# Start-up of a recurrent attention and two MLP layers on one core: set-up, gate rows and sigmoids in other places of the order

## The chip, the cores and the metric
One core of a Trainium2 chip runs the kernel. The metric is the device time of one execution in microseconds (us); the time before is 479.1 us, the median of three runs from 477.7 to 480.66. TensorE is called PE, VectorE DVE, ScalarE ACT, GpSimd POOL, and SyncE, which issues all the transfers here, SP.

## The reference, cut to what matters
For 2 batches, 8 heads, 768 time steps and head size 40, a gated recurrence gives `y`; its 1536 rows of 320 numbers pass through two MLP layers with 2048 hidden units each.

```python
for t in range(S):                                   # attention
    m_new = np.maximum(f_gate[:, :, t] + m, i_gate[:, :, t])
    f_stab, i_stab = np.exp(f_gate[:, :, t] + m - m_new), np.exp(i_gate[:, :, t] - m_new)
    C = f_stab * C + i_stab * outer(v_t, k_t)
    n = f_stab * n + i_stab * k_t
    y[:, :, t] = sigmoid(o_gate[:, :, t]) * (C @ q_t) / np.maximum(np.abs(n @ q_t), 1.0)
x = y.transpose(0, 2, 1, 3).reshape(B * S, H * D)
h = x @ w_in;   x = (h - np.tanh(h)) @ w_out         # layer 0
h = x @ w_in2;  out = (h * np.tanh(softplus(h))) @ w_out2   # layer 1
```

The inputs are float32, but the weights come as 64-bit numbers, which the kernel itself converts.

## The kernel before, in words
**Attention** is done in chunks of 128 time steps: 6 chunks of 2 batches give 12 token tiles j, two tiles to a block. `attention(j)` is a generator that yields between its steps: two halves of exponents of decays (Exp, L304) from PSUM, a POOL product `wv` (L316), two halves of scores (PE L321, DVE L323), the state product `it` for later chunks, the value product `pv` (L341), and then on DVE the denominator (L349 to L351) and the gated output in `xo` (L353, L354). `xo` must hold the sigmoid of the output gate by then. `transpose_x` turns two finished tiles into `xT` (PE L246, ACT L248, DVE L249), the input of layer 0.

**The gates** are rows of 16 partitions (one for each batch and head) by 768 steps: `n_t` and `i_t` (called a in the change) come from DVE scans (L396, L404). They are split into two float parts in `nr` (L434 on ACT, L435 on DVE), from which small transfers (L269, L275) fill rows of `md` and `sd`, the operands of the decay product for chunks past the first (L301). `sd`, `md` and the state `C` are first set to constants by POOL. `u_t` (L442 on POOL) and its Exp give `uT` and `dec` through PE.

**Weights** come in 16 pieces f for each layer. `conv_w` converts one: DVE L175, L176, ACT L177, DVE L178 (the third pass), ACT L179, and then L181 and L182 for the low part, on POOL for the first two pieces and on DVE for the others. The first three pieces of layer 0 have buffers of their own; later ones share three raw buffers, so a new piece is loaded when an older one is converted.

**Layer 0** goes in tiles of two weight pieces: `mm1` (L493), `tile1` (two tanh and Square on ACT, L519, L520 and L522 on DVE, the split into `gh` and `gl`), `mm2` (L552 to L554). For the first block pieces 0 to 7 are converted one after the other while the tiles use them; `conv_to` asks for them ahead. `ahead` advances the attention of the next blocks between tiles.

**Order**: a planner orders each engine's instructions from the order in the program and its own time estimates. `after(x)` adds an order on one engine behind the instructions in `x`, with no wait of its own. `session(c0, c1)` puts output-gate sigmoids behind every Exp and Tanh so far (`texp`) and then a dummy Exp (L626), behind which later Exp and Tanh come (`tbl`). So it holds ACT for two table loads and the sigmoids. Session (0, 2) is in the first block; session (2, 6) stands in `attend`, at the seventh step of the second block. PE runs dummy products (`spin`, L592) in gaps of the start.

Of the kernel before, what the change touches and what calls it, by code (L numbers as in the profile page):

```python
# [8 lines left out]
F32 = mybir.dt.float32  # L9
# [16 lines left out]
def kernel(  # L26
# [11 lines left out]
    nc = tc.nc  # L38
# [89 lines left out]

    texp, tbl, dls = [], [], []

    spq, cvd, hold = [], [], []

    def after(x):
        e = ExitStack()
        for i in x:
            e.enter_context(tc.issue_after(i.ins))
        return e
# [25 lines left out]
                    spq[:] = [x]  # L163
                raw[layer, f] = t

    def conv_w(layer, f):
        r = raw.pop((layer, f)).rearrange("p (n t) -> p n t", t=2)
        lo32, z = r[:, :, 0], r[:, :, 1]
        zf = z.bitcast(F32)
        w = wp.tile([P, WT], F32R, tag="w", name="w")  # L170
        wf = w.bitcast(F32)

        nc.vector.tensor_scalar(lo32, in0=lo32, scalar1=29, scalar2=None, op0=ALU.logical_shift_right)  # L175
        nc.vector.scalar_tensor_tensor(lo32, in0=z, scalar=0x80000000, in1=lo32, op0=ALU.bitwise_and, op1=ALU.bitwise_or)  # L176
        scaled[layer, f] = nc.scalar.activation(out=zf, in_=zf, func=AF.Copy, scale=2.0 ** -111)  # L177
        nc.vector.scalar_tensor_tensor(z, in0=z, scalar=3, in1=lo32, op0=ALU.logical_shift_left, op1=ALU.bitwise_or)  # L178
        cvd[:] = [nc.scalar.activation(out=w[:, 0:WC], in_=zf, func=AF.Copy)]  # L179
        eng = nc.gpsimd if layer == 0 and f < PRE else nc.vector  # L180
        eng.tensor_tensor(w[:, WC:WT], in0=zf[:, 0:REM0], in1=wf[:, 0:REM0], op=ALU.subtract)  # L181
        eng.tensor_tensor(w[64:P, REM0:REM1], in0=zf[64:P, REM0:REM1], in1=wf[64:P, REM0:REM1], op=ALU.subtract)  # L182
        wtile[layer, f] = w
# [77 lines left out]
    def attention(j):  # L261
# [55 lines left out]
        for hf in range(2):  # L317
            sc = at_ps([P, 4, L], "sc")
            for hh in range(4):
                h = 4 * hf + hh  # L320
                x = nc.tensor.matmul(sc[:, hh, :], lhsT=hp(kT, h, HP), rhs=hp(q, h, HP), start=True, stop=True)  # L321
            d4 = Dm[:, 4 * hf:4 * hf + 4, :]
            nc.vector.tensor_tensor(d4, in0=sc, in1=d4, op=ALU.mult)  # L323
            yield
        hv = ap_.tile([P, H, D1], F32, tag="hv", name="hv", bufs=2) if c else None
        hs = slice(b * H, (b + 1) * H)
# [18 lines left out]
        else:  # L345
# [8 lines left out]
        nc.vector.scalar_tensor_tensor(  # L354
            x, in0=x, scalar=1 / WS, in1=den.to_broadcast([P, H, D]), op0=ALU.mult, op1=ALU.mult
        )
        copy_r(0, xo[:, j, DM:3 * P], xo[:, j, 2 * P:DM])
# [22 lines left out]
    def gates():  # L380
# [9 lines left out]
        nc.vector.memset(ch(rm)[:, :, 0:1], 0.0)  # L390
        nc.gpsimd.memset(na[0].bitcast(F32), 0.0)
        nc.gpsimd.memset(g_t, 0.0)
        nc.gpsimd.tensor_tensor(sel, in0=ident[:, 0:BH], in1=ident[:, 32:32 + BH], op=ALU.add)

        def scans(a, e):
# [27 lines left out]
        first = parts(0)  # L423

        def rest():
            nc.gpsimd.memset(ch(u_t)[:, 0:1, :], 0.0)
            with after([first]):
                scans(L, S)
            return rest_u

        def rest_n():
            for n, t in enumerate((n_t, i_t)):
                t, hi, lo = t[:, EC * L:S], nr[64 * n:64 * n + BH], nr[64 * n + 32:64 * n + 32 + BH]
                copy_r(0, hi, t)  # L434
                nc.vector.tensor_tensor(lo, in0=t, in1=hi.bitcast(F32), op=ALU.subtract)  # L435

        def rest_u():
            mp = once.tile([BH, NCH, 1], F32, name="mp")
            nc.vector.tensor_tensor(
                mp[:, 1:NCH, :], in0=ch(n_t)[:, 0:NCH - 1, L - 1:L], in1=ch(F_t)[:, 0:NCH - 1, L - 1:L], op=ALU.add  # L440
            )
            dls[:] = [nc.gpsimd.tensor_tensor(  # L442
                ch(u_t)[:, 1:NCH, :], in0=ch(n_t)[:, 1:NCH, :], in1=mp[:, 1:NCH, :].to_broadcast([BH, NCH - 1, L]),
                op=ALU.subtract,
            )]
            return rest_t

        def rest_t():
            with after(tbl):
                nc.scalar.activation(out=u_t, in_=u_t, func=AF.Exp, scale=-1.0)  # L450
            u_ps = at_ps([P, NCH, BH], "u_ps")
            for c in range(NCH):
                nc.tensor.transpose(u_ps[:, c, :], ch(u_t)[:, c, :], ident[0:BH, 0:BH])
            nc.vector.tensor_copy(uT, u_ps)

            ue = once.tile([BH, BH, NCH], F32, name="ue")
            nc.vector.tensor_tensor(
                ue, in0=ident[0:BH, 0:BH].rearrange("p (h o) -> p h o", o=1).to_broadcast([BH, BH, NCH]),
                in1=ch(u_t)[:, :, L - 1].rearrange("p (o c) -> p o c", o=1).to_broadcast([BH, BH, NCH]), op=ALU.mult,
            )  # L460
# [7 lines left out]
            return rest_n  # L468

        return rest, first  # L470

# [113 lines left out]
    def program():  # L585
# [16 lines left out]
        for x in "qkqkOwOw":  # L602
# [7 lines left out]

        big = cm.bitcast(F32)
        nc.gpsimd.memset(big, 0.0)
        nc.gpsimd.affine_select(
            out=cm, in_=big, pattern=[[1, L]], base=0, channel_multiplier=-1, compare_op=ALU.is_ge, fill=2.0 ** 100
        )
        copy_r(0, identr, ident)
        for n, v_ in enumerate((-G_T,)):
            nc.vector.memset(bias[:, n:n + 1], v_)
# [13 lines left out]
        def go(g, n=1):  # L632
            for _ in range(n):
                next(g, 0)

        go(ga, 4)
        go(gb, 4)
        session(0, 2)
        go(ga)
        go(gb)  # L640
        with after(dls):
            for t in Cst:
                nc.gpsimd.memset(t, 0.0)
        go(ga)
        go(gb)
        loads_to(2 * B, "qk")
# [10 lines left out]

        def lead1(n, x=()):
            while conv1[0] < min(n, NF):
                with after(x):  # L660
                    conv_w(0, conv1[0])
                if conv1[0] >= PRE:
                    load_w()
                if conv1[0] == PRE + 1:
                    with after(spq):
                        load_o(*oc.pop(0))
                conv1[0] += 1


        with after(dls):  # L670
            for b, t in enumerate(sds):
                f = t.bitcast(F32)
                nc.gpsimd.memset(f, 0.0)
                nc.gpsimd.affine_select(
                    out=t, in_=f, pattern=[[0, P]], base=-b, channel_multiplier=1, compare_op=ALU.not_equal, fill=1.0
                )
                nc.gpsimd.affine_select(
                    out=t, in_=f, pattern=[[0, P]], base=-B - b, channel_multiplier=1, compare_op=ALU.not_equal, fill=1.0
                )
            nc.gpsimd.memset(md_.bitcast(F32), 0.0)  # L680
            mf = md_.bitcast(F32)
            for n in range(2):
                nc.gpsimd.affine_select(
                    out=md_, in_=mf, pattern=[[-HG, 2], [-1, HG], [0, L]], base=-K0 - H * n, channel_multiplier=1,
                    compare_op=ALU.not_equal, fill=-1.0,
                )
        spq[:] = kvd
        lead1(1)
        rest = rest()
        rest = rest()  # L690
        rest = rest()
        lead1(PRE)
        at_pools[:] = [(ps_acc, "acc")] * PS[0] + [(ps_at, "at")] * PS[2]


        def attend():
            for k in range(1, NB):
                js, n_st = blk[0, k], 0
                gens = [(n, attention(j)) for n, j in enumerate(js)]
                if k < NB - 1:  # L700
                    new_xT(0, k)
                loads_to(js[0] + 1)
                while gens:
                    for n, g in list(gens[:2]):
                        loads_to(js[n] + 2)
                        n_st += 1
                        if k == 1 and n_st == 7:
                            session(2, NCH)
                        if next(g, 0) == 0:
                            gens.remove((n, g))  # L710
                            if k < NB - 1:
                                yield
                                transpose_x(0, k, n)
                        yield
            left.close()
            late["x"] = pool(left, "lateX", 1, reuse_waits="tile")
            late["A"] = pool(left, "lateA", 2, reuse_waits="tile")
            yield from trans(0, NB - 1)
# [52 lines left out]
        for i in range(len(tiles)):  # L771
# [25 lines left out]
            mm1(i)  # L797
            if l == 0:
                tile1(i)
                qm.append(i)  # L800
                if len(qm) > LAG:
                    mm2(qm.pop(0))
# [77 lines left out]
```

## Time and profile before

| | |
|---|---|
| median of 3 runs | 479.1 us |
| the profiled execution | 479.02 us |
| its span | 476.9 us |
| PE busy | 459.6 us (96%) |
| DVE busy | 320.7 us (67%) |
| ACT busy | 283.9 us (60%) |
| POOL busy | 119.5 us (25%) |
| mean granted clock of PE | 0.978 |

The span is what the trace covers; 2.1 us of the execution's time lie around it. Busy PE includes dummy products and work at half clock, so its share is no measure of useful work.

### The profile page before, as it was taken

To read this page: it belongs to the slowest core of one execution; us is meant where nothing else is said; L and a number is where in the kernel's file an instruction comes from. 1 tells how busy PE (TensorE), PEld (TensorE's weight loads), DVE (VectorE), ACT (ScalarE), POOL (GpSimd) and SP (SyncE) were. 2 spreads that over 40 slices of the span, in tenths; PEclk is the share of its full clock that TensorE was granted. 3 is DMA by queue.
4 is the path that set the end of the run, shared out by engine and by line. 5 is a ranking of instruction groups with operands and counts; after the bars stand their busy time and mean duration, and the time that the engine had idled before them with its cause. 6 is when DMAs were issued, how large, how long until landed. Compare 5 with 4: busy or idle time off the path is not lost.

```text
span 476.9 us, 8013 instructions
## 1 busy us (share of the span) xinstructions
PE 459.6 (96%) x3103; PEld 418.2 (88%) x3103; DVE 320.7 (67%) x544; ACT 283.9 (60%) x513; POOL 119.5 (25%) x132
## 2 busy tenths in 40 slices
PE   9868999999999999999999998999999999999996
PEld 5536898999999989999999887989989998998895
DVE  7889588998968888666899897789942321121111
ACT  3776837567576675797987675866744322332231
POOL 2912526427464252243332333100000000000000
PEclk9997959999999999999999999999999999999999
DMA  7954161542513321000101101055401000010001
GB/s 256 375 197 147 58 219 45 179 136 65 177 33 105 101 63 62 0 1 2 61 12 51 62 1 63 21 205 173 149 0 56 1 1 1 0 56 0 1 0 55
DMA packets 22745, 38.04 MB, mean 80 GB/s; under 512 B 1364, under 2 KB 17044, under 8 KB 22708
## 3 DMA queue, kind: packets, MB, share of 16 engines
q1 hardware_dynamic: 22708, 37.54, 23.8%
q8 instruction: 24, 0.39, 0.3%
q14 instruction: 13, 0.11, 0.1%
HBM read 35.41 MB, written 1.97 MB: 78 GB/s over the span
## 4 chain that ended last, share of the span: by engine, by line
PE 77%; DVE 8%; issue 5%; ACT 3%; DMA 3%; POOL 2%; ACTq 0%; DVEq 0%; POOLq 0%; SPq 0%
PE h L493 32%; PE acc L554 10%; PE acc L552 10%; PE acc L553 10%; PE sc L321 4%; PE pv L341 4%; DMA raw<-in_w_dram 3%; POOL gl L506 2%; PE it L330 2%; PE xt L246 1%; PE st L362 1%; DVE raw L176 1%; PE w_ps L592 1%; DVE g L522 1%; DVE raw L175 1%
## 5 line engine op out<-in xcount | busy, mean ns | idle before, releaser
L493 PE MATMUL h<-xT,w 128*128 128x256 f32 (+1 forms) x1152 | 212.3, 325 | 7.8 <-ACT w L179 3.4
L493 PEld LDWEIGHTS h<-xT,w 128*128 128x128 f32 x1152 | 170.8, 191 | 24.8 <-ACT w L179 4.0
L552 PE MATMUL acc<-w,gh 128*128 128x320 f32 x384 | 120.2, 315 | 1.3 <-ACT gh L141 0.8
L553 PE MATMUL acc<-w,gh 128*128 128x320 f32 x384 | 118.9, 312 | 0.0
L554 PE MATMUL acc<-w,gl 128*128 128x320 f32 x384 | 110.5, 312 | 0.1
L506 POOL TENSOR_TENSOR gl<-g,gh 128x512 fp32r<-128x512 f32 x48 | 66.5, 1386 | 137.9 <-ACT gh L141 124.0
L535 DVE TENSOR_TENSOR gl<-g,gh 128x512 fp32r<-128x512 f32 x48 | 33.1, 691 | 85.7 <-ACT g L534 85.7
L552 PEld LDWEIGHTS acc<-w,gh 128*128 128x128 f32 x384 | 73.0, 190 | 5.3 <-issue 1.3
L553 PEld LDWEIGHTS acc<-w,gh 128*128 128x128 f32 x384 | 72.8, 190 | 2.3
L533 ACT ACTIVATE gh<-h 128x512 fp32r<-128x512 f32 x48 | 28.8, 601 | 75.5 <-PE h L493 75.4
L554 PEld LDWEIGHTS acc<-w,gl 128*128 128x128 f32 x384 | 69.9, 189 | 1.8 <-POOL gl L506 0.3
L141 ACT ACTIVATE gh<-g 128x512 fp32r<-128x512 f32 x48 | 30.4, 634 | 29.8 <-DVE g L522 22.3
L522 DVE COPY_PREDICATED g<-u,t 128x512 f32<-128x512 uint32 x48 | 41.0, 855 | 7.5 <-ACT u L521 7.3
L519 DVE TENSOR_TENSOR g<-u,h 128x512 f32<-128x512 f32 x48 | 32.7, 681 | 14.7 <-ACT u L518 11.5
L521 ACT ACTIVATE u<-u,bias 128x512 f32<-128x512 f32 x48 | 34.9, 727 | 10.5 <-DVE g L519 10.4
L178 DVE SCALAR_TENSOR_TENSOR raw<-raw 128x704 uint32<-128x704 uint32 x32 | 34.5, 1082 | 7.5 <-ACT raw L177 7.3
L179 ACT ACTIVATE w<-raw 128x704 fp32r<-128x704 f32 x32 | 27.8, 875 | 16.0 <-DVE raw L178 15.9
L516 ACT ACTIVATE u<-h 128x512 f32<-128x512 f32 x48 | 28.4, 591 | 14.4 <-PE h L493 14.3
L177 ACT ACTIVATE raw<-raw 128x704 f32<-128x704 f32 x32 | 27.7, 867 | 9.3 <-DVE raw L176 8.3
L520 DVE TENSOR_TENSOR t<-h,t 128x512 f32<-128x512 f32 x48 | 32.8, 684 | 0.0
L176 DVE SCALAR_TENSOR_TENSOR raw<-raw 128x704 uint32<-128x704 uint32 x32 | 30.3, 948 | 0.3
L518 ACT ACTIVATE u<-u 128x512 f32<-128x512 f32 x48 | 30.5, 636 | 0.0
(105 smaller groups left out, 503.2 us busy)
## 6 DMA issues: line engine op xcount, KB each, us to landing
raw<-in_w_dram SPq DMA_DIRECT2D x32, 704.0 KB
qk_t<-in_qk_dram SPq DMA_DIRECT2D x12, 512.0 KB
kv_t<-in_kv_dram SPq DMA_DIRECT2D x12, 324.0 KB
out_dram<-xo SPq DMA_DIRECT2D x12, 160.0 KB
xo<-in_og_dram SPq DMA_DIRECT2D x2, 640.0 KB
xo<-in_og_dram SPq DMA_DIRECT2D x2, 320.0 KB
sd<-nr SPq DMA_DIRECT2D x20, 4.0 KB
md<-nr SPq DMA_DIRECT2D x10, 8.0 KB
```

The source lines that it names most:

```text
L176: nc.vector.scalar_tensor_tensor(lo32, in0=z, scalar=0x80000000, in1=lo32, op0=ALU.bitwise_and, op1=ALU.bitwise_or)
L178: nc.vector.scalar_tensor_tensor(z, in0=z, scalar=3, in1=lo32, op0=ALU.logical_shift_left, op1=ALU.bitwise_or)
L493: y = nc.tensor.matmul(t[:, k * nt:(k + 1) * nt], lhsT=w[:, o:o + P], rhs=x[:, kk, :], start=(n == 0), stop=(n == len(pairs) - 1),)
L506: nc.gpsimd.tensor_tensor(gl, in0=g, in1=gh.bitcast(F32), op=ALU.subtract)
L519: mark[:] = [nc.vector.tensor_tensor(g, in0=u, in1=h, op=ALU.mult)]
L520: nc.vector.tensor_tensor(t, in0=h, in1=t, op=ALU.subtract)
L521: nc.scalar.activation(out=u, in_=u, func=AF.Relu, bias=bias[:, 0:1])
L522: nc.vector.copy_predicated(out=g, mask=u.bitcast(U32), data=t)
L535: nc.vector.tensor_tensor(gl, in0=g, in1=gh.bitcast(F32), op=ALU.subtract)
L552: nc.tensor.matmul(a, lhsT=gh[:, sl], rhs=wh, start=(f in ends_), stop=False)
L553: nc.tensor.matmul(a, lhsT=gh[:, sl], rhs=wl, start=False, stop=False)
L554: nc.tensor.matmul(a, lhsT=gl[:, sl], rhs=wh, start=False, stop=(f + 1 in ends_ or f == NF - 1))
```

## The change
- In `program`, POOL's constants for `sd`, `md` and `C` follow the mask `cm` at once, and the zeros of `u_t` are written before it. Before, they followed the first block's `wv`.
- `rest()` is called three times between the two first tiles' attention; it now does the scans, then the two-part rows `nr`, then `u_t`. The last part, `rest_t` (Exp of `u_t`, `uT`, `dec`), takes the place that `nr` had, behind the first block's `xT`. The ACT copies of `nr` stand behind the first tile's Exp, its DVE differences behind the first tile's scores (`scored[0]`), and `u_t` on POOL behind the first `wv`.
- For pieces 0 and 1 the third pass L178 stands behind the gated output of tile 0 and 1 (`gated`), and the first pass of piece 1 behind the third pass of piece 0.
- `session(2, NCH)` moves from `attend` to directly behind `tile1(0)`.

```diff
-    def conv_w(layer, f):
+    def conv_w(layer, f, first=(), behind=()):
...
-        nc.vector.tensor_scalar(lo32, in0=lo32, scalar1=29, ...)
+        with after(first):
+            nc.vector.tensor_scalar(lo32, in0=lo32, scalar1=29, ...)
...
-        nc.vector.scalar_tensor_tensor(z, in0=z, scalar=3, in1=lo32, ...)
+        with after(behind):
+            third[layer, f] = nc.vector.scalar_tensor_tensor(z, in0=z, scalar=3, in1=lo32, ...)
...
         def rest():
-            nc.gpsimd.memset(ch(u_t)[:, 0:1, :], 0.0)
             with after([first]):
                 scans(L, S)
-            return rest_u
+            return rest_n
...
-                copy_r(0, hi, t)
-                nc.vector.tensor_tensor(lo, in0=t, in1=hi.bitcast(F32), op=ALU.subtract)
+                with after(texp):
+                    copy_r(0, hi, t)
+                with after([scored[0]]):
+                    nc.vector.tensor_tensor(lo, in0=t, in1=hi.bitcast(F32), op=ALU.subtract)
+            return rest_u
...
+        for b, t in enumerate(sds):          # memset and two affine_select for each, behind the mask
+        ...                                  # the same for md_ and the memsets of Cst
...
         go(ga, 4)
+        rest = rest()
+        rest = rest()
+        rest = rest()
         go(gb, 4)
         session(0, 2)
...
-        with after(dls):
-            for t in Cst:
-                nc.gpsimd.memset(t, 0.0)
...
+                f = conv1[0]
                 with after(x):
-                    conv_w(0, conv1[0])
+                    conv_w(0, f, [third[0, f - 1]] if f and f < PRE else (), [gated[f]] if f < PRE else ())
...
-        with after(dls):
-            for b, t in enumerate(sds):      # and md_, as above
...
-        lead1(1)
-        rest = rest()
-        rest = rest()
-        rest = rest()
         lead1(PRE)
...
-                        if k == 1 and n_st == 7:
-                            session(2, NCH)
...
             if l == 0:
                 tile1(i)
+                if not i:
+                    session(2, NCH)
```

## Rows read from the trace of the kernel before
**Rows 1.** The page's slices: granted clock of PE, in tenths, 40 slices
```profile
PEclk9997959999999999999999999999999999999999
```
**Rows 2.** Busy us (instructions) of PE, PEld, DVE, ACT, POOL; clock, DMA share, GB/s
```profile
27.50:45.00 17.50, 12.30 (x57) 8.51 (x57) 16.96 (x26) 11.47 (x19) 1.28 (x1) 0.80 0.30 99
31.20:43.50 12.30, 7.11 (x29) 5.30 (x30) 12.14 (x18) 8.18 (x13) 1.28 (x1) 0.72 0.14 45
59.60:73.40 13.80, 13.80 (x84) 12.85 (x82) 11.79 (x31) 4.62 (x9) 2.76 (x3) 0.51 0.63 195
80.00:476.00 396.00, 389.44 (x2666) 364.38 (x2664) 256.44 (x428) 233.96 (x430) 86.17 (x82) 1.00 0.18 57
```
**Rows 3.** DVE in order of time, start to first `xT`: start, us, instruction, idle before
```profile
2.82 0.41 DVE L396 TENSOR_TENSOR_SCAN gF<-grm,gf 16x128 f32<-16x128 f32 x1 [0.73 <-DMA gf<-in_fg_dram]
...
9.51 1.29 DVE L323 TENSOR_TENSOR Dm<-sc,Dm 128x512 f32<-128x512 f32 x2 [0.18 <-PE sc L321]
12.53 0.53 DVE L175 TENSOR_SCALAR raw<-raw 128x704 uint32<-128x704 uint32 x1 [1.72 <-DMA raw<-in_w_dram]
...
14.31 1.27 DVE L323 TENSOR_TENSOR Dm<-sc,Dm 128x512 f32<-128x512 f32 x2
17.23 1.91 DVE L178 SCALAR_TENSOR_TENSOR raw<-raw 128x704 uint32<-128x704 uint32 x1 [1.64 <-ACT raw L177]
...
19.59 0.15 DVE L349 TENSOR_SCALAR den<-pv 128x8 f32<-128x8 f32 x1
...
21.22 1.03 DVE L354 SCALAR_TENSOR_TENSOR xo<-xo,den 128x320 f32<-128x320 f32 x1
...
23.83 0.62 DVE L457 TENSOR_TENSOR ue<-ident,gu 16x96 f32<-16x96 f32 x1
24.38 0.47 DVE L354 SCALAR_TENSOR_TENSOR xo<-xo,den 128x320 f32<-128x320 f32 x1
...
26.95 0.56 DVE L249 TENSOR_TENSOR xT<-xt,xT 128x384 fp32r<-128x384 f32 x1 [0.22 <-ACT xT L248]
```
**Rows 4.** DVE in order of time, after the first `xT`
```profile
28.41 0.81 DVE L435 TENSOR_TENSOR nr<-n_all,nr 16x640 fp32r<-16x640 f32 x1
...
32.28 0.89 DVE L178 SCALAR_TENSOR_TENSOR raw<-raw 128x704 uint32<-128x704 uint32 x1
...
58.42 0.89 DVE L178 SCALAR_TENSOR_TENSOR raw<-raw 128x704 uint32<-128x704 uint32 x1 [3.40 <-ACT raw L177]
```
**Rows 5.** The chain that ended last, at the second session: start, us, what
```profile
51.27 1.28 ACT L222
```
**Rows 6.** PE in order of time: `pv` of the first two tiles
```profile
13.19 1.98 PE L341 MATMUL pv<-kv_t,Dm 128*128 128x41 f32 x16
...
15.91 1.98 PE L341 MATMUL pv<-kv_t,Dm 128*128 128x41 f32 x16
```
**Rows 7.** POOL: the first `dl`, the last set-up instruction, and a stretch (columns of rows 2)
```profile
8.98 0.20 POOL L145 TENSOR_SCALAR dl<-Dm 128x8 f32<-128x8 f32 x1 [6.08 <-ACT Dm L304]
...
22.64 1.63 POOL L683 TENSOR_SCALAR_AFFINE_SELECT md<-md 128x1024 fp32r<-128x1024 f32 x1
...
13.59:20.11 6.52, 6.52 (x72) 4.94 (x71) 4.88 (x7) 4.43 (x6) 6.23 (x14) 1.00 1.11 347
```
**Rows 8.** ACT in order of time: Exp, tanh of the first tile, the second session
```profile
10.76 0.60 ACT L304 ACTIVATE Dm<-nb 128x512 f32<-128x512 f32 x1 [1.86 <-PE nb L295]
...
31.40 0.59 ACT L517 ACTIVATE t<-h 128x512 f32<-128x512 f32 x1
...
52.56 2.62 ACT L222 ACTIVATE xo<-xo 128x640 f32<-128x640 f32 x4
55.19 1.28 ACT L626 ACT_TABLE_LOAD   x1
```
**Rows 9.** SP: the last output gates' transfers; the stretch (columns of rows 2) in which they end
```profile
20.95 0.98 SPq L217 DMA_DIRECT2D xo<-in_og_dram  x2
...
30.00:31.00 1.00, 1.00 (x7) 0.44 (x5) 0.97 (x2) 0.81 (x2) 0.00 (x0) 1.00 0.13 41
```

More of the change, by code (lines that the diff above doesn't have):

```diff
@@ L129 @@
     texp, tbl, dls = [], [], []
+    scored, gated = {}, {}
     spq, cvd, hold = [], [], []
@@ L164, in load_w @@
                 raw[layer, f] = t
-    def conv_w(layer, f):
+    third = {}
+    def conv_w(layer, f, first=(), behind=()):
         r = raw.pop((layer, f)).rearrange("p (n t) -> p n t", t=2)
@@ L171, in conv_w @@
         wf = w.bitcast(F32)
-        nc.vector.tensor_scalar(lo32, in0=lo32, scalar1=29, scalar2=None, op0=ALU.logical_shift_right)
+        with after(first):
+            nc.vector.tensor_scalar(lo32, in0=lo32, scalar1=29, scalar2=None, op0=ALU.logical_shift_right)
         nc.vector.scalar_tensor_tensor(lo32, in0=z, scalar=0x80000000, in1=lo32, op0=ALU.bitwise_and, op1=ALU.bitwise_or)
         scaled[layer, f] = nc.scalar.activation(out=zf, in_=zf, func=AF.Copy, scale=2.0 ** -111)
-        nc.vector.scalar_tensor_tensor(z, in0=z, scalar=3, in1=lo32, op0=ALU.logical_shift_left, op1=ALU.bitwise_or)
+        with after(behind):
+            third[layer, f] = nc.vector.scalar_tensor_tensor(
+                z, in0=z, scalar=3, in1=lo32, op0=ALU.logical_shift_left, op1=ALU.bitwise_or
+            )
         cvd[:] = [nc.scalar.activation(out=w[:, 0:WC], in_=zf, func=AF.Copy)]
@@ L322, in attention @@
             d4 = Dm[:, 4 * hf:4 * hf + 4, :]
-            nc.vector.tensor_tensor(d4, in0=sc, in1=d4, op=ALU.mult)
+            scored[j] = nc.vector.tensor_tensor(d4, in0=sc, in1=d4, op=ALU.mult)
             yield
@@ L353, in attention @@
         nc.vector.tensor_tensor(x, in0=hv[:, :, 0:D], in1=x, op=ALU.mult)
-        nc.vector.scalar_tensor_tensor(
+        gated[j] = nc.vector.scalar_tensor_tensor(
             x, in0=x, scalar=1 / WS, in1=den.to_broadcast([P, H, D]), op0=ALU.mult, op1=ALU.mult
@@ L392, in gates @@
         nc.gpsimd.memset(g_t, 0.0)
+        nc.gpsimd.memset(ch(u_t)[:, 0:1, :], 0.0)
         nc.gpsimd.tensor_tensor(sel, in0=ident[:, 0:BH], in1=ident[:, 32:32 + BH], op=ALU.add)
@@ L441, in rest_u @@
             )
[L442 to L445, printed above, removed]
+            with after(dls):
+                nc.gpsimd.tensor_tensor(
+                    ch(u_t)[:, 1:NCH, :], in0=ch(n_t)[:, 1:NCH, :], in1=mp[:, 1:NCH, :].to_broadcast([BH, NCH - 1, L]),
+                    op=ALU.subtract,
+                )
             return rest_t
@@ L467, in rest_t @@
             nc.vector.tensor_copy(dec, d_ps)
-            return rest_n
         return rest, first
@@ L612, in program @@
         nc.gpsimd.memset(big, 0.0)
-        nc.gpsimd.affine_select(
+        masked = nc.gpsimd.affine_select(
             out=cm, in_=big, pattern=[[1, L]], base=0, channel_multiplier=-1, compare_op=ALU.is_ge, fill=2.0 ** 100
         )
+        for b, t in enumerate(sds):
+            f = t.bitcast(F32)
+            with after([masked]):
+                nc.gpsimd.memset(f, 0.0)
+            nc.gpsimd.affine_select(
+                out=t, in_=f, pattern=[[0, P]], base=-b, channel_multiplier=1, compare_op=ALU.not_equal, fill=1.0
+            )
+            nc.gpsimd.affine_select(
+                out=t, in_=f, pattern=[[0, P]], base=-B - b, channel_multiplier=1, compare_op=ALU.not_equal, fill=1.0
+            )
+        with after([masked]):
+            nc.gpsimd.memset(md_.bitcast(F32), 0.0)
+        mf = md_.bitcast(F32)
+        for n in range(2):
+            nc.gpsimd.affine_select(
+                out=md_, in_=mf, pattern=[[-HG, 2], [-1, HG], [0, L]], base=-K0 - H * n, channel_multiplier=1,
+                compare_op=ALU.not_equal, fill=-1.0,
+            )
+        with after([masked]):
+            for t in Cst:
+                nc.gpsimd.memset(t, 0.0)
         copy_r(0, identr, ident)
@@ L659, in lead1 @@
             while conv1[0] < min(n, NF):
+                f = conv1[0]
                 with after(x):
-                    conv_w(0, conv1[0])
+                    conv_w(
+                        0, f, [third[0, f - 1]] if f and f < PRE else (), [gated[f]] if f < PRE else ()
+                    )
                 if conv1[0] >= PRE:
@@ L667, in lead1 @@
                 conv1[0] += 1
-        with after(dls):
-            for b, t in enumerate(sds):
[L672 to L686, printed above, removed]
         spq[:] = kvd
-        lead1(1)
-        rest = rest()
-        rest = rest()
-        rest = rest()
         lead1(PRE)
@@ L697, in attend @@
             for k in range(1, NB):
-                js, n_st = blk[0, k], 0
+                js = blk[0, k]
                 gens = [(n, attention(j)) for n, j in enumerate(js)]
@@ L705, in attend @@
                         loads_to(js[n] + 2)
-                        n_st += 1
-                        if k == 1 and n_st == 7:
-                            session(2, NCH)
                         if next(g, 0) == 0:
```

## The prediction
> **What bounds the kernel now.** I read the page's slices first. The granted clock is full but for slices 4 and 6 [rows 1], so there is something to find in the first 80 us. The table of stretches says the same: from 80 us on PE is busy 389.44 of 396 us at clock 1.00 [rows 2]. What the start loses or wins is passed on to the end, as long as that later stage stays bound by PE. All parts of the change lie before 60 us.
>
> The start has three stages. Up to 27.51 us the kernel makes the first block's `xT`; its last step is the DVE pass at 26.95 [rows 3]. From 27.5 to 45 us DVE is busy 16.96 of 17.50 us [rows 2]: it converts weight pieces 2 to 5, with the first tile's work in between, and PE waits for it. At 51.27 the chain of waits goes through ACT's table load of the second session [rows 5]. That session lasts from 51.27 to about 56.7 us, with sigmoids of 2.62 and a second load of 1.28 [rows 8]. Behind it a weight pass comes late on ACT, and DVE's third pass at 58.42 stands still for 3.40 us for it [rows 4]. After that PE is fully busy from 59.6 to 73.4 at a granted clock of 0.51, the 1.2 GHz level [rows 2].
>
> **The set-up.** POOL idles for 6.08 us before the first `dl` at 8.98 [rows 7]. Moving the set-up there costs POOL at most 6.23 + 1.63 = 7.9 us by the stretch and the last select [rows 7]; the first figure includes the `u_t` row, so the real load is less. If it overran, `dl` and `wv` of the first tile would be up to 1.8 us late. The first `wv` is needed only by products behind `pv`, which ends at 15.2 [rows 6], so I cost it at nothing. If POOL were slower still, PE's state products and the key-value buffers behind them would be late. The gain is that POOL is clear when it converts the low parts of pieces 0 and 1, and that DVE's weight passes there no longer run beside it: the third pass took 1.91 us at 17.23 beside the set-up and 0.89 us at 32.28 without [rows 3, 4].
>
> **Two-part rows.** ACT's two copies of `nr` can use its 1.86 us idle before 10.76 [rows 8]. The two DVE differences (0.81 us each, one row shown) fit the 1.72 us that DVE waits at 12.53 for the first weight piece [rows 3, 4]. They leave the DVE-bound stretch, which gets `rest_t` instead: 0.62 for the product with the identity [rows 3] and two smaller copies that I bound by 0 and 0.62; its Exp moves to where ACT has idle time. The stretch gains 0.4 to 1.0 us; I take 0.6. `u_t` on POOL stands behind the first `wv` and fits before the second. The small transfers of `md` and `sd` become ready early; SP could put them ahead of weight loads, but DVE is not short of weight pieces then, so nothing.
>
> **First x ahead of the third passes.** DVE ends the second tile's scores at 15.58, then waits 1.64 us for ACT and runs the third pass of piece 0 for 1.91 us [rows 3]. Tile 0's `pv` was done at 15.17 [rows 6], yet its denominator starts only at 19.59 [rows 3]. With the third pass behind the gated output, the denominator can start at 15.6. From L349 to the end of L354 took 19.59 to 22.25, 2.66 us, with one weight pass of about 0.89 inside, so 1.8 us alone: tile 0 is gated at 17.4 instead of 22.25. The third pass then ends at 18.3 (0.89). Tile 1 (`pv` at 17.89 [rows 6]) takes another 1.8 and is gated at 20.1, or at 21.5 if piece 1's first two passes (0.53 and about 0.89) go in between. From gated tile 1 to the end of `xT` took 24.85 to 27.51, 2.66 us [rows 3]. So `xT` ends between 22.8 and 24.2; I take 23.0, since the first passes fill gaps between dependent steps. **Gain 4.5 us**, with 0 (the low parts of piece 1 hold the first tile as long as before) and 5.2 as ends.
>
> **The session.** Away from 51.27 it frees at least the 3.40 us of DVE's wait [rows 4] and at most its whole 5.4 us (1.28 + 2.62 + 1.28 and the dummy); I take the middle, 4.4. In its new place behind the first tile's tanh it takes the same 5.4 us from ACT. From 31.2 to 43.5 ACT is busy 8.18 of 12.30 us [rows 2], so 4.1 us of idle can take most of it. At best 1.3 us are left over, at worst all 5.4, if none of the idle time falls right, since weight passes queue behind it on ACT and DVE waits for them. DVE has passes of other pieces and of the tile to run meanwhile, so I take 2.4, nearer the good end. Net gain 2.0 us, from -2.0 to 4.1.
>
> The Trainium skill, page ScalarE: Activation LUTs, section What ACT_TABLE_LOAD costs, speaks against moving two table switches into a full stretch: it counts a load of 1283 ns and a drain of about 1380 ns for each switch. Here the first sigmoid starts 1.29 us after the load's start [rows 5, 8], so the load is seen and the drain is not. By the page the insertion would cost 2.7 us more (two drains), an estimate, and the sum would be about 474.7.
>
> **Sum.** 4.5 + 0.6 + 2.0 = 7.1 us from the profiled execution's 479.02, which stands 0.1 below the median: **472 us**. The half-clock stretch at 59.6 is taken as it is, since what PE is fed there keeps its order.
>
> **Rivals.**
> A. **The clock stays up.** PE enters the stretch at 59.6 after thin products (the value products) and a short wait for the late weights. If those are ready, the h products fill that time and the clock may not fall. PE is busy 13.80 us there at half clock [rows 2], so up to 6.9 us come back: 465 us. For it: the same kind of products later run at 1.00. Against it: the clock has already fallen once, in slice 4, and could at any other place.
>
> B. **Given back in the middle.** The sigmoids need the last output gates. Their transfers were issued at 20.95 and DMA engines fall idle only in the microsecond after 30 [rows 9]. If tanh of the first tile ends 4.5 earlier than 31.99 [rows 8], at 27.5, and the table load follows at once, ACT stands until about 30.1, some 1.3 us, and then the session costs its full 5.4, with only 3.4 won later: 479.0 - 5.1 - 3.4 + 5.4 + 1.3 = 477 us. For it: DVE has no idle time in that stretch to absorb late passes. Against it: ACT's copies for weights may pass between.
>
> C. **Slower: PE starves and its clock falls for longer.** As B, but the longer wait for weights between 27 and 40 us leaves PE idle. A second half-clock stretch as long as that at 59.6 then lies over the attention of the second block: 477.2 + 6.9 = 484 us. It decides when ACT's block is so long that PE is still at 1.2 GHz once its work becomes dense, at about 44 us. For it: slice 4, where the clock fell after PE had waited for weights. Against it: there the clock was back before the dense work.
>
> D. **POOL beside the scans.** The scans start at 2.82 and end just before 9.5 [rows 3], and the set-up now runs beside them. The only row for such a pairing is the third pass, 1.91 against 0.89 us [rows 3, 4]; the scans have no such row. If DVE lost half of some 5.4 us, the first scores, the differences and the first weight passes would be 2.6 us late, and so would x: 472 + 2.6 = 474.6 us.
>
> The Trainium skill, page GPSIMD Engine Reference, section 8. Key points, says that GpSimd shares its SBUF interfaces with VectorE and contends with instructions that have two SBUF inputs; the scans are of this kind. The row of the third pass agrees, but no run here shows a scan beside the set-up.
>
> **How the numbers follow.** Forecast 0.46, A 0.17, B 0.18, C 0.12, D 0.07. The forecast's own range is 467 to 475.5. Less than 1% (4.8 us, below 474.3 or above 483.9) can't be told from no change. The forecast lies nearly all below 474.3 (0.41 of 0.46). With A and a part of D (0.03) faster has 0.61. The rest of the forecast, B and the rest of D give 0.27 for no change, and C gives 0.12 for slower. The range goes from 464 (A with its margin) to 480 (no x gain beyond 1.5 us and the bad end of the session: 479.0 - 1.5 - 0.6 + 2.0 = 479); C lies outside, with little else.
>
> **What would show it.** Right: the second `xT` pass ends at about 23 us, not 27.5; the first tanh ends 4 to 5 us earlier; the third pass of piece 0 takes about 0.9 us and stands behind L354; the load of the second session lies between 27 and 33 us; no wait of 3.40 us on DVE before the last third pass of pieces up to 7; the scans last what they did (0.41 us for the first). Wrong: sigmoids that wait for their transfers with ACT idle before them (B), a granted clock of 0.5 for more than 14 us of dense PE work (C) or none after 50 us (A), scans clearly longer (D), or a later stage in which PE idles more than the 6.6 us it idles now after 80 us.

## The result, and the profile after

The changed kernel takes 472.94 us, the median of four runs from 472.48 to 474.19, against 478.4 us for the kernel before in the same job. The ratio is 0.9877 with an interval of 0.9839 to 0.9915. The profiled execution took 472.48 us, with a span of 470.4 us and a mean granted clock of 0.992. The forecast was 472 us, with a range of 467 to 475.5 of its own.

The page of the changed kernel, first the granted clock in 40 slices of 11.8 us, then the engines:

```profile
PEclk9997999999999999999999999999999999999999
...
PE 455.7 (97%) x3103; PEld 412.7 (88%) x3103; DVE 321.7 (68%) x544; ACT 284.1 (60%) x513; POOL 121.2 (26%) x132
```

The dip of slice 4 is still there, at the 1.2 GHz level for a part of it (0.50 from 35 to 40 us); the one of slice 6 [rows 1] is gone. Next the stretches of the changed kernel, with columns as in [rows 2]:

```profile
27.50:45.00 17.50, 13.20 (x63) 8.20 (x62) 15.14 (x26) 16.27 (x25) 1.49 (x2) 0.80 0.51 174
31.20:43.50 12.30, 8.92 (x35) 5.71 (x35) 10.00 (x16) 12.26 (x19) 1.28 (x1) 0.72 0.37 123
59.60:73.40 13.80, 12.55 (x106) 10.43 (x106) 13.47 (x28) 7.80 (x15) 6.63 (x7) 1.00 0.47 147
80.00:470.40 390.40, 383.22 (x2615) 358.48 (x2613) 248.23 (x421) 231.40 (x427) 81.71 (x76) 1.00 0.18 58
25.93:71.00 45.07, 39.44 (x267) 30.70 (x268) 42.28 (x71) 30.96 (x52) 15.99 (x20) 0.92 0.55 184
```

Against [rows 2]: ACT is now busy 12.26 of 12.30 us where the session went, PE has 106 products instead of 84 from 59.6 to 73.4 and does them at clock 1.00, and from 80 us on PE stands still for 7.2 us (6.6 before). The last line has no counterpart there. It runs from the end of the first block's `xT` to the start of the last DVE pass of the second block's `xT`. The same stretch of the kernel before:

```profile
27.51:76.05 48.54, 42.41 (x246) 34.70 (x246) 40.58 (x71) 30.72 (x51) 12.97 (x16) 0.79 0.40 130
```

Both do 71 DVE instructions there. The first block's `xT` ends 1.58 us earlier, DVE stands still for 2.79 instead of 7.96 us, and is busy 1.70 us longer: 1.58 + 5.17 - 1.70 = 5.05, and the second block's `xT` ends at 71.54 instead of 76.61. This is an account of one profiled execution of each kernel, not yet a cause. What follows this `xT` lasts 398.9 us after and 400.3 before. So **5.1 of the 6.5 us of span come from the time up to the second block's `xT`, and most of that from DVE's idle time between the two**. DVE's waits in that stretch (engine, line, releaser: us, times, longest), the kernel before:

```profile
DVE raw L178 <- ACT raw L177: 3.4, 1, 3.4
DVE Dm L323 <- POOL dl L145: 1.5, 1, 1.5
DVE hv L344 <- PE pv L341: 1.2, 1, 1.2
DVE raw L175 <- DMA raw<-in_w_dram: 0.7, 1, 0.7
DVE C L370 <- PE st L362: 0.6, 1, 0.6
```

and the changed kernel:

```profile
DVE raw L184 <- ACT raw L182: 2.1, 1, 2.1
```

The wait behind the session got shorter, and the four others are gone. DVE's instructions of the changed kernel in order of time (start, us, instruction, idle before; L184 was L178, L362 was L354, L257 was L249):

```profile
3.73 1.20 DVE L410 TENSOR_SCALAR n<-gi 16x128 fp32r<-16x128 f32 x1
...
5.56 1.06 DVE L427 TENSOR_TENSOR n<-n_all,n 32x128 fp32r<-32x128 f32 x1
6.65 1.48 DVE L405 TENSOR_TENSOR_SCAN gF<-grm,gf 16x640 f32<-16x640 f32 x1
...
8.91 1.05 DVE L412 COPY gg<-gF 16x5 f32<-16x5 f32 x1
...
9.99 1.54 DVE L413 TENSOR_TENSOR_SCAN n_all<-gg,n_all,gi 16x640 f32<-16x640 f32 x1
...
17.46 0.15 DVE L357 TENSOR_SCALAR den<-pv 128x8 f32<-128x8 f32 x1
...
18.35 0.49 DVE L362 SCALAR_TENSOR_TENSOR xo<-xo,den 128x320 f32<-128x320 f32 x1
19.12 0.89 DVE L184 SCALAR_TENSOR_TENSOR raw<-raw 128x704 uint32<-128x704 uint32 x1 [0.27 <-ACT raw L182]
...
21.99 1.02 DVE L362 SCALAR_TENSOR_TENSOR xo<-xo,den 128x320 f32<-128x320 f32 x1
...
25.37 0.56 DVE L257 TENSOR_TENSOR xT<-xt,xT 128x384 fp32r<-128x384 f32 x1 [0.81 <-ACT xT L256]
...
40.84 0.89 DVE L184 SCALAR_TENSOR_TENSOR raw<-raw 128x704 uint32<-128x704 uint32 x1 [2.14 <-ACT raw L182]
...
62.89 0.49 DVE L352 TENSOR_TENSOR hv<-hv,pv 128x328 f32<-128x328 f32 x1
...
64.92 0.49 DVE L362 SCALAR_TENSOR_TENSOR xo<-xo,den 128x320 f32<-128x320 f32 x1
...
71.00 0.54 DVE L257 TENSOR_TENSOR xT<-xt,xT 128x384 fp32r<-128x384 f32 x1
```

The order that the change asks for is there: the gated output of tile 0 ends at 18.84, then the third pass, in 0.89 us. But the gated output of tile 1 ends at 23.01 and `xT` at 25.93, so of the 4.5 us that were forecast 1.6 came. ACT shows a part of the reason (changed kernel, same columns):

```profile
11.56 0.74 ACT L143 ACTIVATE nr<-n_all 16x640 fp32r<-16x640 f32 x1 [2.23 <-DVE n_all L413]
...
13.08 1.09 ACT L312 ACTIVATE Dm<-nb 128x512 f32<-128x512 f32 x2
14.19 1.28 ACT L230 ACT_TABLE_LOAD   x1
...
30.73 0.59 ACT L528 ACTIVATE t<-h 128x512 f32<-128x512 f32 x1
...
34.68 1.28 ACT L230 ACT_TABLE_LOAD   x1
35.97 2.62 ACT L230 ACTIVATE xo<-xo 128x640 f32<-128x640 f32 x4
```

The copies of `nr` wait 2.23 us for the scan, and the second tile's Exp stands behind them and starts at 13.08 instead of 10.76 [rows 8]. The first session then starts at 14.19 instead of 12.27. The first tanh ends 0.7 us earlier than before, and the second session has moved to 34.68.

### The profile page after: what moved, and what is told of

Read it like the earlier page. It is cut to its first block, busy times and chain, and to the rows that moved or that the text cites. A ratio compares the mean times of both kernels' runs of the same rounds, so it can differ in the third digit from the quotient of the medians.

```text
span 470.4 us, 8021 instructions
## 1 busy us (share of the span) xinstructions
PE 455.7 (97%) x3103; PEld 412.7 (88%) x3103; DVE 321.7 (68%) x544; ACT 284.1 (60%) x513; POOL 121.2 (26%) x132
## 4 chain that ended last, share of the span: by engine, by line
PE 74%; DVE 11%; issue 6%; ACT 4%; DMA 2%; POOL 2%; ACTq 0%; DVEq 0%; POOLq 0%; SPq 0%
PE h L504 32%; PE acc L563 10%; PE acc L565 10%; PE acc L564 10%; PE sc L329 4%; PE pv L349 3%; POOL gl L517 2%; DMA raw<-in_w_dram 2%; PE it L338 1%; PE xt L254 1%; DVE raw L181 1%; DVE raw L180 1%; PE st L370 1%; DVE g L530 1%; DVE t L531 1%
## 5 line engine op out<-in xcount | busy, mean ns | idle before, releaser
L184 DVE SCALAR_TENSOR_TENSOR raw<-raw 128x704 uint32<-128x704 uint32 x32 | 32.2, 1009 | 2.8 <-ACT raw L182 2.6
L181 DVE SCALAR_TENSOR_TENSOR raw<-raw 128x704 uint32<-128x704 uint32 x32 | 30.0, 940 | 0.3
```

Of the source, the lines that this page charges most:

```text
L184: third[layer, f] = nc.vector.scalar_tensor_tensor(z, in0=z, scalar=3, in1=lo32, op0=ALU.logical_shift_left, op1=ALU.bitwise_or)
```

## The experiments

Each ratio is to the kernel before in the same job, with a 95% interval. They ran in three jobs, in which the kernel before had medians of 479.28 (e1, e2, e3, e5), 479.81 (e4, e6, e7, e8) and 478.8 us (e9, e11, e12, e13).

**e1: the changed kernel with the session where it was.**
```diff
+                        if k == 1 and n_st == 7:      # in attend
+                            session(2, NCH)
...
                 tile1(i)
-                if not i:
-                    session(2, NCH)
```


> The changed kernel with the second session back at its old step of the second block's attention; set-up, rows and third passes stay moved. Theory T (most of the gain is the second half-clock stretch that went away, and the session brought that): the session stands again before the last weight passes, PE is again at about 0.5 of its clock for some 10 to 14 us around 57 to 73 us, and the time is 476 to 478 us. Rival R (the sum as predicted: 4.5 + 0.6 us from the start stages, 2.0 from the session): 474 us, whatever the clock does.

475.5 us, 0.9918 [0.9885, 0.9951]. Beside 0.9877 for the whole change, the move of the session is worth 0.0041, or 2.0 us, on top of the rest; the intervals overlap, so this size is not settled. PE's clock is down again, as Theory T said: 0.50 from 60 to 66 us. The time is 3.8 us below the kernel before all the same, between what T and R gave.

**e2: the kernel before with the session behind `tile1(0)`, and nothing else.** The same edit, the other way round.

> The kernel before with the second session alone moved behind the first tile's tanh. Theory T: no half-clock stretch after 50 us, 473 to 475 us. Rival R: 2.0 us gained, 477 us.

478.44 us, 0.9973 [0.9952, 0.9994]: some 1.3 us by itself. In its profile DVE's wait for ACT only changed place: a low-part pass now waits 2.8 us for ACT's second pass of a piece, which stands behind the session. The granted clock is 1.00 from 57 to 73 us, yet the 473 to 475 us of Theory T do not come with it.

**e3: the changed kernel with POOL's set-up late, as before.**
```diff
-        for b, t in enumerate(sds): ...     # and md_, Cst, behind the mask
...
+        with after(dls):                    # behind the first block's wv
+            for t in Cst: ...
...
+        with after(dls):
+            for b, t in enumerate(sds): ... # and md_
```


> The changed kernel with POOL's set-up of sd, md and C back behind the first wv products; all else stays moved. Theory T with POOL contention: the short DVE passes at 3.7, 5.6 and 8.9 us (1.20, 1.06, 1.05 us in the changed kernel) fall to about 0.2 to 0.3 us, the second scan ends near 9.5 instead of 11.5 us, ACT's copies of the rows no longer hold the second tile's Exp, and the first session starts near 12.3 instead of 14.2 us; the first xT ends 1 to 2 us earlier unless the set-up then slows the gating passes. Time 470.5 to 473. Rival R (the set-up beside the scans costs nothing): the scans end where they do now, near 11.5 us, and the time is 472.5 us or more, since POOL is then late for the low weight parts.

472.21 us, 0.9847 [0.9805, 0.9888]. Beside the other parts, the early set-up is worth nothing measurable. DVE of e3, to be held against the changed kernel's rows of L410, L427, L412 and L413:

```profile
3.73 0.21 DVE L410 TENSOR_SCALAR n<-gi 16x128 fp32r<-16x128 f32 x1
...
4.88 0.28 DVE L427 TENSOR_TENSOR n<-n_all,n 32x128 fp32r<-32x128 f32 x1
...
7.45 0.15 DVE L412 COPY gg<-gF 16x5 f32<-16x5 f32 x1
7.64 1.54 DVE L413 TENSOR_TENSOR_SCAN n_all<-gg,n_all,gi 16x640 f32<-16x640 f32 x1
```

Without POOL beside them the short passes take 0.21, 0.28 and 0.15 instead of 1.20, 1.06 and 1.05 us; the long scan takes 1.54 in both. The scans end at 9.18 instead of 11.53. But the late set-up then runs beside the first weight passes: L180 at 14.01 takes 2.09 us, against 0.53 in the changed kernel, and L181 at 16.61 takes 1.69 against 0.88. The first `xT` of e3 ends at 28.54, later than in any kernel but e2, and its time is as good: the first `xT` does not set the time.

**e5: the kernel before with four dummy products ahead of the third token tile's value products**, into `pv`, which those overwrite.
```diff
         pv = at_ps([P, H, D1], "pv")
+        if (b, c) == (0, 1):
+            for _ in range(4): nc.tensor.matmul(...)    # bf16, 32x328
...
```


> The kernel before with four dummy products (32x328, bf16) on PE ahead of the value products of the third tile, at about 56.8 us, and the order of all engines up to there as it was. Theory T: the fall of the clock at 59.5 us comes from the thin products and the short wait in front of it; with the dummies the clock stays at 1.00, the stretch from 59.6 to 73.4 shortens, and the time falls by 4 to 6 us to 473 to 475 us although work was only added. Rival R (the half-clock stretch costs nothing that isn't lost elsewhere, or the dummies don't hold the clock): 479 to 480 us.

479.01 us, 0.9989 [0.9964, 1.0013]. The clock did stay up. Stretches of e5, columns as above:

```profile
59.60:73.40 13.80, 11.08 (x105) 9.81 (x104) 13.48 (x32) 5.97 (x13) 2.24 (x4) 1.00 0.72 228
70.00:74.00 4.00, 1.54 (x9) 1.13 (x9) 3.90 (x9) 2.40 (x5) 0.21 (x1) 1.00 0.29 83
```

PE got through 105 products instead of 84 at full clock and then ran dry: from 70 to 74 it is busy 1.54 of 4.00 us while DVE is busy 3.90. Against the kernel before, DVE's idle time up to the second `xT` fell by 3.5 us, but its busy time rose by 2.2 and the first `xT` came 0.9 us later (table below): the second `xT` ends 0.3 us earlier. The orders of DVE, ACT and POOL are the same in both up to 60 us, so the 0.9 us do not come from these; a milestone of a single profile may move by that much. PE busy at half clock [rows 2] hid how little DVE had to spare.

**e6: the changed kernel without the order of x ahead of the third passes.**
```diff
-                    conv_w(0, f, [third[0, f - 1]] if f and f < PRE else (), [gated[f]] if f < PRE else ())
+                    conv_w(0, f)
```


> The changed kernel without the order of the third passes of pieces 0 and 1 behind the gated outputs, and without that of piece 1's first pass. Rival R (the sum as predicted): the part worth 4.5 us is gone, 477 us. Theory S: it is worth 1.6 us at most, as the first xT ended only 1.6 us earlier in the changed kernel: 472.5 to 474.5.

474.06 us, 0.9871 [0.9813, 0.9929]. The first `xT` ends at 27.30, 1.4 us later, and the time is the same. The term that I priced highest is worth nothing as long as the other parts are there.

**e7: the changed kernel with the two-part rows and `u_t` in their old place and order.**
```diff
...                                  # inside `rest`: the old sequence, no `after`
         go(ga, 4)
-        rest = rest()
-        rest = rest()
-        rest = rest()
         go(gb, 4)
...
         spq[:] = kvd
+        lead1(1)
+        rest = rest()
+        rest = rest()
+        rest = rest()
         lead1(PRE)
```


> The changed kernel with the two-part rows, u_t and its Exp back at their old places; set-up early, third passes and session as changed. Rival R (the sum as predicted): 0.6 us lost, 473.5 us. Theory S: the rows' 1.6 us of DVE work is back in the full stretch, and ACT's copies no longer hold the second tile's Exp: between 473 and 476 us, so most of what the front brings hangs on this part.

480.57 us, 1.0010 [0.9978, 1.0042]. The part that I had priced at 0.6 us takes the whole gain with it, though the first `xT` ends at 26.09, as early as in the changed kernel. ACT of e7:

```profile
35.33 1.28 ACT L230 ACT_TABLE_LOAD   x1
...
40.65 0.81 ACT L187 ACTIVATE w<-raw 128x704 fp32r<-128x704 f32 x1
```

Here the session stands ahead of the second ACT pass of piece 3 (40.65); in the changed kernel it stands behind it. DVE's low-part passes behind it are the last to read that piece's raw buffer, so the load of piece 6 is issued at 42.63, against 37.98.

**e9: e7 with the session also behind that pass.**
```diff
                 if not i:
-                    session(2, NCH)
+                    with after(cvd):
+                        session(2, NCH)
```


> The kernel with the rows back at their old place (e7), with the second session also ordered behind the last ACT pass of weight piece 3. Theory M (the session costs by which weight passes stand behind it on ACT: in e7 piece 3's second ACT pass waited for the session, its buffer came free at 42.6 instead of 38.0 us, and pieces 6 and 7 were loaded that much later): the load of piece 6 is issued at 39 to 41 us and the time is 474 to 477 us, against 480.6 for e7. Rival N (the early rows matter by their own DVE time or by their early transfers): 479 us or more.

477.09 us, 0.9959 [0.9932, 0.9986]: 0.0051, or 2.4 us, better than e7, with intervals that just overlap. The load of piece 6 goes out at 39.72. So the late load, or something else that moved with the session, is a part of what e7 lost, and not the larger one.

**e11: the changed kernel with the session one tile later**, so that no weight pass up to piece 5 stands behind it.
```diff
+            if i == 1:
+                with after(cvd):
+                    session(2, NCH)
             mm1(i)
```


> The changed kernel with the second session behind the ACT passes of pieces 4 and 5, ahead of the second tile's tanh. Theory M: piece 4 is done on DVE before 41 us instead of 43.7, the load of piece 7 is issued 3 us earlier, and the time is 1 to 4 us below the changed kernel: 469 to 472 us. Rival N (the place of the session among the weight passes doesn't matter, the second tile's tanh and the Exp behind it do): 473 us or more, as they stand behind the session then.

482.4 us, 1.0078 [1.0034, 1.0123]. The loads of pieces 6 to 8 go out early, from 37.97 to 42.9, and it is slower than the kernel before all the same. As the main cause, the late load has fallen.

**e4: the changed kernel with the `nr` copies behind the first session's dummy Exp**, to give the second tile's Exp its old start.
```diff
-                with after(texp):
+                with after(tbl):
                     copy_r(0, hi, t)
...
-        rest = rest()
-        rest = rest()
         go(gb, 4)
         session(0, 2)
+        rest = rest()
+        rest = rest()
```


> The changed kernel with ACT's two copies of the gate rows behind the first session's dummy Exp instead of ahead of the second tile's Exp. Theory S (the front's gain is DVE work taken out of its full stretch and passes that no longer run beside POOL; where exactly the first x ends matters little): the first session starts near 12.7 instead of 14.2 us, the first xT ends 0.5 to 1.5 us earlier, and the time is within 1.5 us of the changed kernel: 471.5 to 474. Rival R (each microsecond of an earlier first x comes through, as predicted): 471 to 472, as much below the changed kernel as xT is earlier.

479.08 us, 0.9961 [0.9927, 0.9994]. The first session starts at 12.30, as hoped. But DVE's differences of the rows now wait for the moved copies and stand ahead of the first denominator, which starts at 18.83 instead of 17.46. The first `xT` ends no earlier (26.08), and the time is 4 us worse than the change's; neither theory foresaw that.

**e8: e3 and e4 together.**

> The changed kernel with POOL's set-up late again and ACT's copies of the rows behind the first session: both things that held the first tile's chain are taken away. Theory S: first session near 12.5 us, first xT by 25 us, 470.5 to 472.5. Rival R: as e3 or better by what xT is earlier; a time above 473 would speak against both.

480.1 us, 1.0003 [0.9972, 1.0035], above 473, which speaks against both theories. The scans do end 2.3 us earlier than in e4 (9.19 against 11.54). DVE of e8 behind them:

```profile
16.67 1.89 DVE L445 TENSOR_TENSOR nr<-n_all,nr 16x640 fp32r<-16x640 f32 x1 [0.30 <-ACT nr L143]
18.60 2.12 DVE L445 TENSOR_TENSOR nr<-gi,nr 16x640 fp32r<-16x640 f32 x1
```

POOL's late set-up runs beside the two differences until 20.03, and they take 1.89 and 2.12 us instead of 0.81 [rows 4]. That gives back what the scans had won, so e8 does not tell what the scans' delay is worth.

**e12: the rows and the session alone**, that is e3 with the edit of e6.

> The kernel before with the early rows and the moved session alone: set-up late, no order of the third passes. Theory M: these two carry the whole gain, 472 to 474.5 us. Rival R (the sum as predicted, rows 0.6 and session 2.0): 476.5 us.

480.34 us, 1.0031 [1.0010, 1.0052]. Leaving out the set-up costs nothing (e3), leaving out the order of x costs nothing (e6), and leaving out both costs the whole gain. Both forecasts for e12 failed. Its first `xT` ends at 25.98. DVE of e12 around the fourth token tile, the second of the second block:

```profile
65.70 0.49 DVE L352 TENSOR_TENSOR hv<-hv,pv 128x328 f32<-128x328 f32 x1
66.11 0.95 DVE L180 TENSOR_SCALAR raw<-raw 128x704 uint32<-128x704 uint32 x2
...
68.77 2.78 DVE L181 SCALAR_TENSOR_TENSOR raw<-raw 128x704 uint32<-128x704 uint32 x2
...
72.75 0.17 DVE L358 TENSOR_TENSOR den<-hv,den 128x8 f32<-128x8 f32 x1
72.84 1.69 DVE L184 SCALAR_TENSOR_TENSOR raw<-raw 128x704 uint32<-128x704 uint32 x2
...
74.64 0.76 DVE L189 TENSOR_TENSOR w<-raw,w 128x576 fp32r<-128x576 f32 x1
75.41 0.29 DVE L190 TENSOR_TENSOR w<-raw,w 64x128 fp32r<-64x128 f32 x1
75.73 0.49 DVE L362 SCALAR_TENSOR_TENSOR xo<-xo,den 128x320 f32<-128x320 f32 x1
```

From the add of `pv` (L352) to the end of the gated output (L362) the changed kernel takes 2.5 us (62.89 to 65.41), e12 10.5 (65.70 to 76.22). DVE is busy for 10.31 of these 10.5 us, and 6.5 of them are the passes of pieces 8 and 9 shown above, which no product needs yet. PE waits for the gated output in e12:

```profile
76.37 0.66 PE L254 MATMUL xt<-ident,xo 128*128 128x128 f32 x2 [3.02 <-DVE xo L362]
```

**e13: e3 with the edit of e11.**

> As e11, with POOL's set-up late. Theory M with POOL contention: as e11 or up to 1.5 us less. Rival N: 473 us or more.

483.44 us, 1.0108 [1.0058, 1.0157], the slowest of all. A stretch of e13, columns as above:

```profile
60.00:70.00 10.00, 10.00 (x48) 10.00 (x47) 5.06 (x11) 1.19 (x4) 4.96 (x6) 0.50 0.47 150
```

From 60 to 70 PE, at half clock, is the full engine, and DVE is busy for 5.06 us only. DVE waits for PE there, 4.2 us for the value products of tiles 3 and 4, so in this kernel the half clock does bind.

**All profiles in one table.** "Busy" and "idle" are DVE's, from the end of the first `xT` to the start of the second block's last `xT` pass. "Tile 4" is the time from the add of `pv` to the end of the gated output. The times are us of the profiled execution, and the last column is the span less the end of the second `xT`. Each row is one execution; those of e3 and e13 are the slowest of their kernels (473.91 and 486.9 us).

| kernel | first xT | busy | idle | tile 4 | second xT | rest |
|---|---|---|---|---|---|---|
| after | 25.93 | 42.28 | 2.79 | 2.5 | 71.54 | 398.9 |
| e6 | 27.30 | 40.37 | 3.03 | 2.5 | 71.27 | 401.1 |
| e3 | 28.54 | 40.55 | 2.85 | 2.6 | 72.48 | 399.6 |
| e4 | 26.08 | 42.15 | 5.33 | 2.5 | 74.12 | 402.0 |
| e1 | 27.02 | 42.54 | 5.84 | 3.2 | 75.95 | 398.9 |
| e5 | 28.43 | 42.83 | 4.49 | 3.5 | 76.29 | 399.5 |
| before | 27.51 | 40.58 | 7.96 | 6.2 | 76.61 | 400.3 |
| e2 | 29.92 | 39.18 | 6.99 | 3.3 | 76.63 | 400.1 |
| e8 | 27.99 | 42.36 | 5.79 | 2.5 | 76.70 | 402.3 |
| e9 | 25.63 | 46.76 | 5.07 | 10.4 | 78.02 | 397.0 |
| e12 | 25.98 | 46.86 | 6.22 | 10.5 | 79.62 | 398.3 |
| e7 | 26.09 | 45.67 | 8.34 | 9.4 | 80.69 | 398.2 |
| e11 | 25.93 | 45.71 | 8.96 | 9.9 | 81.12 | 399.5 |
| e13 | 28.43 | 45.31 | 10.30 | 9.9 | 84.60 | 400.5 |

Where the second `xT` ends ranges over 13.3 us, what follows it over 5.3. So the span follows the second `xT` in the main, but not to the microsecond: of the 5.7 us of span that e4 is longer than the changed kernel, 2.6 lie before it and 3.1 behind. The first `xT` alone says little of the time: e12 has one of the earliest, e3 one of the latest. Two things go with a late second `xT`: DVE's idle time, and its busy time, 45.3 to 46.9 us in the five kernels whose tile 4 takes over 9 us and 39.2 to 42.8 in the others. The five have 46 weight passes on DVE before it, the others 38 to 40.

**What stays open.** That the early passes of pieces 8 and 9 are the cause in those five kernels fits the profiles, but no run isolates it: holding them behind the fourth tile's gated output, and nothing else, was not tried. Why the planner puts them there in e12 and not in e3 or e6 was not looked into either. Nor does a run isolate DVE's idle time, which is most of what the change itself won.

## Why the prediction was right, and which steps of it were not

**The number was right by luck.** The sum was 4.5 for x, 0.6 for the rows and 2.0 for the session; 5.5 us between the medians was measured. But without the largest term the time is the same (e6), and without the smallest nothing of the gain is left (e7), so the runs do not bear the sum out as a sum. Of the signs that I gave for being right, three failed: the first block's `xT` ended at 25.93 and not near 23, the first tanh 0.7 us earlier and not 4 to 5, and the session's load stood at 34.68 and not between 27 and 33. One sign of being wrong came, weakly: PE stands still for 7.2 us after 80, not 6.6.

**What is won at the start is passed on: right in the main**, for another milestone than mine. In the change 5.1 us of span are won up to the second `xT` and 1.4 behind it, and the stretch from 80 us on looks as it did [rows 2]. Over all kernels the table's last column varies by 5.3 us, so it is no strict rule.

**First x, 4.5 us: the step that failed.** It was the sum of "tile 0 is gated at 17.4" and "gated at 20.1, or at 21.5". Measured were 18.84 and 23.01. The step put the first denominator at 15.6, right behind the second tile's scores; it started at 17.46, as these scores were late. The scans ended 2.4 us later than in e3, the two differences did not fall into the 1.72 us of waiting for a weight piece but ran from 13.31 to 14.98 ahead of the second tile's scores, and the copies of `nr`, for which I had used ACT's idle time before 10.76 [rows 8], could only start when the scan had ended, at 11.53, and pushed the second tile's Exp to 13.08. Then piece 1's first two passes stood between third pass and second gated output, as in the 21.5 of the text and not in the 20.1. What each of these is worth alone is open, since e4 and e8 put other work in the way. Only 1.6 us were left, and e6 shows that the time does not depend on them. The first tanh ended 0.7 us earlier, and from there ACT is the fuller engine: 16.27 of 17.50 us against DVE's 15.14.

**The rows, 0.6 us: wrong in size and kind.** Without their new place nothing is left of the gain (e7). It is not their own duration, 1.6 us for the two differences: DVE's busy time up to the second `xT` grows by 3.4 us and its idle time by 5.6. The profile of e7 has another order behind them, with the session ahead of piece 3 and weight passes inside tile 4. I priced an edit by its instructions; most of what it did came through the order of others.

**The session, 2.0 us: right in sign, and the size fits**, by e1 (2.0 on top of the rest, with intervals that overlap) and e2 (1.3 alone). The mechanism was nearly the one given: the wait of 3.40 us [rows 4] went, and one of 2.14 us came behind the session's new place, where I had taken 2.4.

**The set-up at nothing: right beside the other parts** (e3), but not without the order of x: e12 is e6 with the set-up late, and takes 1.0031 instead of 0.9871. POOL of the changed kernel:

```profile
5.39 1.09 POOL L642 TENSOR_SCALAR_AFFINE_SELECT md<-md 128x1024 fp32r<-128x1024 f32 x1
...
8.19 1.75 POOL L642 TENSOR_SCALAR_AFFINE_SELECT md<-md 128x1024 fp32r<-128x1024 f32 x1
9.91 0.20 POOL L147 TENSOR_SCALAR dl<-Dm 128x8 f32<-128x8 f32 x1
10.20 1.87 POOL L324 TENSOR_TENSOR wv<-kv_t,dl 128x328 f32<-128x328 f32 x1
```

The first `dl` is 0.93 us later than in [rows 7], within the 1.8 us allowed for. The third pass did become 0.89 us, as said, but **rival D** took that back elsewhere. D came in its kind, and nearly in its size of 2.6 us: the two long scans kept 1.48 and 1.54 us, while four shorter instructions around them, the first short scan among them (1.06 us against 0.41 in e3), grew to over 1 us, and the scans ended 2.4 us later. In e3 they end at 9.18, but the late set-up then holds up weight passes, and the time is the same.

**Rival A** came with half of what it said. The granted clock was 1.00 from 59.6 to 73.4, and the time stayed above 472 instead of falling towards 465. That the gain is nothing but the clock, an obvious rival, is spoken against by three runs: in e5 and e2 the clock stayed at 1.00 there for 0 and 1.3 us, and in e1 it fell while 3.8 us were won. The clock may still have helped beside the other parts; no run holds it alone at half in the changed kernel.

**Rival B** did not come. The session's load at 34.68 shows no wait for the output gates: their transfers had landed, as the DMA engines had fallen idle by 34 us. **Rival C** did not come with the change. e13 has a part of it: PE is fully busy at half clock from 60 to 70. That its 483.44 us lie near C's 484 shows nothing, as C's sum was for another order, and the kernel before has 13.8 us at half clock [rows 2].

## What to carry to other kernels

In a kernel whose order is planned, an edit can act less by its own instructions than by how it reorders those behind it, so gains taken one at a time need not add: here two parts were each worth nothing to leave out and the whole gain together. Look for the milestone that the end follows at a nearly constant distance (here the second block's `xT`, 397 to 402 us before the end, while it moves by 13.3 us itself), and not for the first one that the edit moves; then read which instructions stand between its steps on the in-order engine. A stretch of PE at half clock may hide another engine's bound, as from 59.6 us in the kernel before, and then a faster clock returns nothing (e5); in e13 it hides none.

## What the runs showed of the hardware

Beside POOL's set-up, short DVE instructions took up to 1 us longer, with one source (L410 1.20 us against 0.21 in e3, L412 1.05 against 0.15) and with two (L427 1.06 against 0.28; in e8 the differences L445 1.89 and 2.12). Each of the three short ones ended within 0.2 us of the end of what POOL ran beside it: L427 at 6.62, POOL's select at 6.48; L412 at 9.96, the next select of this kind at 9.94; L410 at 4.93, POOL's constants for `C` at 4.86. The two long scans kept 1.48 and 1.54 us, and beside the second one it was POOL that took longer: the first `wv`, at 10.20, 1.87 us against 0.74 in e3. So in these rows it looks as if one engine waited until the other had ended its instruction; POOL's times in a profile are rough, and no run was made to test it. The Trainium skill, page GPSIMD Engine Reference, section 8. Key points, names VectorE instructions in a 2-port perf mode or with two SBUF inputs as those that contend with GpSimd. The rows with two sources agree; whether the passes with one source ran in such a mode, no run here shows.

In the changed kernel the first sigmoid starts at 35.97, 0.01 us after its table load of 1.28 us ends, in a full stretch of ACT. ACT's instruction before the load ends at 34.66, 0.02 us ahead of it. So the drain of about 1380 ns that speaks against the session's move (the Trainium skill, page ScalarE: Activation LUTs, section What ACT_TABLE_LOAD costs) is not seen there either.
